# Attention and gated MLP on one core: fixed uses for the three transposition banks, weight conversions in other steps, the first x loaded two steps later

## The chip, the cores and the metric

The kernel runs on one core of a Trainium2 chip. The metric is the device time of one execution in microseconds. The core has five engines that run side by side and meet through semaphores: TensorE (PE in the profile; PEld are its weight loads), VectorE (DVE), ScalarE (ACT), GpSimd (POOL) and SyncE (SP), which here issues DMAs only.

## The reference

Attention over 4 batches, 8 heads, 576 positions and head dimension 64, with a bias that a small MLP makes of relative positions; then a gated MLP from 512 to 2048 and back over the 2304 tokens. All inputs are float32, except that the kernel is handed the two MLP weights as 64-bit words, which it converts on the chip.

```python
scores = scale * np.matmul(q, k.transpose(0, 1, 3, 2))
h = np.maximum(x @ w1 + b1, 0.0)            # x: psi_rel / psi_i
scores = scores + (h @ w2).transpose(2, 0, 1)[None, :, :, :]
attn = np.exp(scores - np.max(scores, axis=-1, keepdims=True))
attn = attn / (np.sum(attn, axis=-1, keepdims=True) + 1e-09)
attn_out = np.matmul(attn, v)
h = x @ w_in                                # x: attn_out as (2304, 512)
sp = np.where(h > 20.0, h, np.log1p(np.exp(np.minimum(h, 20.0))))
return (h * np.tanh(sp)) @ w_out
```

## The kernel before

The program has three stages: the bias (until some 56 us of the span), the attention loop (until some 287), and the MLP, in which TensorE is nearly always busy. The change touches the attention loop only.

The loop runs over 16 *pairs*: a pair `i` is one batch and two heads, which lie in the two halves of the 128 partitions. Each pair has five *steps*, one for each block of query rows, in the order 0, 1, 4, 2, 3 of `ORDER` (block 4 is half as long). Below, "first" to "fifth step" is the place in a pair, `x = n % 5` from 0 to 4 in the code; steps 0 to 79 are numbered `n`. Three steps are begun in the bias stage, so the loop proper starts with step 3. Code order is the order in which each engine executes: nothing reorders it (`tc.manual_schedule()`).

Work on one block is spread over several steps:

- `scores(n)`: TensorE, 12 matmuls into two score banks for each of the two heads (4 matmuls in the first three pairs, which are not split into high and low parts). The score banks hold one step only.
- `add_bias(n)`: VectorE, two passes that add the bias, write `pt` and leave the row minimum `m`; they free the score banks.
- `exps(n, u)`: ScalarE, one exponential per head (one for both in the third step, block 4), with the row sums.
- `ends(n)` and `transposes(n)`: TensorE turns `pt` around, 2 transpositions for the last 64 columns (`tail`) and 16 for the rest (`main`; 10 for block 4, which needs no `ends`). They go to `tp_t`, one PSUM tile of three banks. VectorE copies the tail out, ScalarE the two banks of `main` (lines 310, 313, 314).
- `products(n)`: TensorE, 20 matmuls of the transposed block with `v` into the bank `o`; after the second and the fifth block of a pair VectorE copies `o` to `x`, which a DMA writes to `x_d`.

`step(n)` issues `scores(n)`, `add_bias(n)`, `transposes(n-2)`, `exps(n)`, loads (`ahead`), `products(n-3)`, `ends(n-1)`, in a pair's first step the reciprocals of the pair before, and then `split(n)`. So TensorE has `ends(n-1)` right in front of `scores(n+1)`. Steps 3 and 4 are written out differently, as the first three blocks wait there to be transposed.

In `banks_of` the three banks of `tp_t` take turns: each call takes the next ones, so of the two banks that `ends` writes one is that of the first half of the last `transposes`, and the other lay idle.

`split(n)` calls `convert`, which takes one of four parts of a weight's conversion: a multiplication (line 125 on VectorE, or 123 on ScalarE if the weight starts in a third step), a shift (128), and two steps of bit arithmetic (130, 132). When a weight is done, the next is loaded, and the first four are also split in two at once (ScalarE line 142, then GpSimd line 143). Sixteen weights are converted in the loop, in 64 calls: one in each of steps 5 to 24, and later one in each step but the first of a pair.

GpSimd splits the q and k of the next pair (line 177, four subtractions) when their load has landed. In the last pair, `ahead` also makes the MLP's first x ready (lines 381 to 383): `load_x` and `load_r` bring the attention output and the reciprocals of the sums in steps 69 and 70, and steps 75 to 78 multiply them, on VectorE and GpSimd.

Of the kernel before, what the change touches and what calls it, by code (L numbers as in the profile page):

```python
# [7 lines left out]
F32 = mybir.dt.float32  # L8
# [7 lines left out]
B, H, S, D, C = 4, 8, 576, 64, 32  # L16
# [3 lines left out]
P = 128  # L20
# [25 lines left out]
def kernel(ctx: ExitStack, tc, qk, v, wb, w2, w_in, w_out, psia, psi4, rinv, eye, out):  # L46
# [42 lines left out]
    EARLY = 4  # L89
# [122 lines left out]
    NS = len(steps)  # L212
# [59 lines left out]
    def place(c):  # L272
        return (0, c * P) if c < 2 else (1, 0 if c == 4 else 64 + (c - 2) * P)

    tail_t, x_t, n_tp = {}, {}, [0]

    def banks_of(k):
        n_tp[0] += k
        return [(n_tp[0] - k + j) % 3 for j in range(k)]

    def ends(n):
        i, c = steps[n]
        tail_t[n] = tail = ptp.tile([P, P], F32, name="tail")
        if c == 4:
            return
        pt = live[n][0]
        t, l = sorted(banks_of(2))
        for rows, bank in ((TOP, t), (LOW, l)):
            pe.transpose(tp_t[:, bank, 0:64], pt[rows, 512:640], ident[rows, rows])  # L289
        dve.tensor_copy(tail.rearrange("p (g q) -> p g q", g=2), tp_t[:, t:l + 1:l - t, 0:64])  # L290

    def transposes(n, shared=False):
        i, c = steps[n]
        pt = live[n][0]
        main = ptp.tile([P, 2, 4, P], F32, name="main")
        pt_t[n] = main
        top, low = (tp_t[:, bank] for bank in banks_of(2))
        if c < 4:
            cols = [h * 640 + k * P for h in range(2) for k in range(4)]
        else:  # L300
            cols = [k * P for k in range(4)] + [S - P]
        for k, c0 in enumerate(cols):
            for rows, tp in ((TOP, top), (LOW, low)):
                if c == 4 and rows == LOW:
                    c0 = 64 + k * P if k < 4 else 0
                pe.transpose(tp[:, k * 64:k * 64 + 64], pt[rows, c0:c0 + P], ident[rows, rows])  # L306
        if c < 4:
            for g, tp in enumerate((top, low)):
                copy = dve.tensor_copy if shared and g else act.copy
                copy(main[:, :, :, 64 * g:64 * g + 64], tp.rearrange("p (h k q) -> p h k q", h=2, k=4))  # L310
        else:
            for h, tp in enumerate((top, low)):
                act.copy(main[:, h, :, 0:64], tp[:, :256].rearrange("p (k q) -> p k q", k=4))  # L313
                act.copy(tail_t[n][(TOP, LOW)[h], 0:64], tp[(LOW, TOP)[h], 256:320])  # L314

    def products(n):
        i, c = steps[n]
        hp, b = divmod(i, B)
        main, tail, vt = pt_t.pop(n), tail_t.pop(n), v_t[i]
        w = P if c < 4 else 64  # L320
        grp, off = place(c)
        if c in (0, 4):
            o_t[0] = o_ps.tile([P, 512], F32, name="o")
        o = o_t[0]
        for k in range(5):
            for h in range(2):
                pe.matmul(o[h * 64:h * 64 + 64, off:off + w], vt[:, h, k, :], main[:, h, k, :w] if k < 4 else tail[:, :w],  # L327
                          start=(k == 0), stop=(k == 4), skip_group_check=True)
        if c == 1:
            x = xs.tile([P, 320], F32, name="x")  # L330
            dve.tensor_copy(x[:, :256], o[:, :256])
            sp.dma_start(out=x_d[b][:, hp, 0:256], in_=x[:, :256])
        elif c == 3:
            x = xs.tile([P, 320], F32, name="x")
            dve.tensor_copy(x, o[:, :320])
            sp.dma_start(out=x_d[b][:, hp, 256:512], in_=x[:, 64:320])
            sp.dma_start(out=x_d[b][:, hp, 512:576], in_=x[:, 0:64])
# [27 lines left out]
    def ahead(n):  # L365
# [4 lines left out]
        c = {(1, 3): 0, (2, 1): 1, (2, 3): 2, (3, 2): 4, (3, 4): 3}.get((i % B, x))  # L370
        if c is not None and i // B + 1 < HP:
            load_bias(i // B + 1, c)
        if n == NS - 11:
            load_x(0, x0.tile([P, HP, TB], F32, name="xraw"))
        if n == NS - 10:
            x_hi[0], x_lo[0] = (xa_t[:, t].bitcast(F32R) for t in range(2))
            load_r(0, x_lo[0].bitcast(F32), 0, HP)
        if NS - 5 <= n < NS - 1:
# [2 lines left out]
            dve.tensor_tensor(hi, x, lo.bitcast(F32), op=ALU.mult)  # L381
            pool.tensor_tensor(x, x, lo.bitcast(F32), op=ALU.mult)
            pool.tensor_tensor(lo, x, hi.bitcast(F32), op=ALU.subtract)

    def split(n):

        i, x = divmod(n, 5)
        for _ in range((1 if n > 4 else 0)):
            convert(x == 2, order[EARLY + 11])

    done = []

# [10 lines left out]
    def step(n):  # L403
        i, x = divmod(n, 5)
        if n < NS:
            scores(n)
        if n == 3:
            ends(0)
            transposes(0, True)
        if n < NS:  # L410
            add_bias(n)
        if n == 4:
            products(0)
        if 4 <= n < NS + LAG:
            transposes(n - LAG)
        if n < NS:
            exps(n, 0)
            if n == 3:
                ends(1)
                transposes(1, True)  # L420
            exps(n, 1)
            ahead(n)
        if n >= 4:
            products(n - LAG - 1)
        if n <= NS:
            ends(n - 1)
        if n and x == 0 and n <= NS:
            reciprocals(i - 1)
        if n < NS and (x or i < 5):
            split(n)  # L430

# [428 lines left out]
```

## Time and profile before

| | |
|---|---|
| three runs | 669.90, 673.06, 673.11 us; median 673.06 |
| profiled execution | 671.56 us, its span 669.8 us |
| busy over the span | TensorE 635.8 us (95%), weight loads 530.0, VectorE 473.3, ScalarE 406.8, GpSimd 151.5 |
| granted TensorE clock, mean | 0.994 of full speed |
| attention loop, 104 to 270 us | TensorE 158.50, VectorE 139.82, ScalarE 145.96 busy of 166.00 |
| last pair, 270 to 290 us | TensorE 18.38, VectorE 17.66, ScalarE 14.12, GpSimd 10.74 busy of 20.00 |

Times in the profile count from the start of the span. Ends of matmuls are modelled, so a busy TensorE is not TensorE at its peak; the pitch from one step's instruction to the next step's is the surer measure. In the loop three engines are all near their limit, so the question at each place is which of them is waited for.

### The profile page before, as it was taken

The numbers are of one execution on the slowest core, as the hardware profiler recorded it, in microseconds if no ns is written. First come the engines' busy times: TensorE is split into PE (matmuls) and PEld (weight loads), VectorE is DVE, ScalarE is ACT, GpSimd is POOL, SyncE is SP. The second block draws the span as 40 slices with busy tenths as digits, with TensorE's granted clock in tenths as the row PEclk, the third lists the DMA queues.
The fourth block names the chain that finished last, engine by engine and source line by source line (L and its number), as shares of the span: only waits on it lengthen the run. The fifth ranks groups of instructions, "written<-read, shape, count | busy, mean of one in ns | idle before, by whom it ended". The sixth has DMA issues, their size and how long they took to land.

```text
span 669.8 us, 15502 instructions
## 1 busy us (share of the span) xinstructions
PE 635.8 (95%) x6132; PEld 530.0 (79%) x6132; DVE 473.3 (71%) x888; ACT 406.8 (61%) x805; POOL 151.5 (23%) x142
## 2 busy tenths in 40 slices
PE   5867999999999999999999999999999999999997
PEld 3214788888888888778888898888888888888886
DVE  7995788888888888924333536236489888888885
ACT  6894889888888888754333334244574444555441
POOL 0000133333222242422102112121253221333320
PEclk9988999999999999999999999999999999999999
DMA  4998486666578749114639687831765445424400
GB/s 146 310 308 252 154 266 207 208 220 210 181 228 255 238 163 273 52 41 144 204 103 268 235 230 210 251 126 66 249 189 157 151 148 154 135 95 129 135 31 32
DMA packets 101064, 119.76 MB, mean 179 GB/s; under 512 B 15616, under 2 KB 77568, under 8 KB 100992
## 3 DMA queue, kind: packets, MB, share of 16 engines
q1 hardware_dynamic: 98688, 110.59, 52.0%
q0 software_dynamic: 1872, 8.09, 4.0%
q8 instruction: 48, 0.79, 0.5%
q14 instruction: 24, 0.20, 0.1%
q10 hardware_dynamic: 432, 0.09, 0.1%
HBM read 79.47 MB, written 39.28 MB: 177 GB/s over the span
## 4 chain that ended last, share of the span: by engine, by line
PE 74%; ACT 7%; DVE 6%; issue 3%; DMA 2%; SPq 0%; ACTq 0%; DVEq 0%
PE h L587 28%; PE s L226 9%; PE y L708 8%; PE h L708 8%; PE o L327 7%; PE tp L306 5%; PE y L709 4%; PE h L709 4%; ACT main L310 3%; PE tp L289 2%; DVE pt L243 2%; ACT main L313 2%; DMA xlo<-r_d 1%; ACT tail L314 1%; DVE w L128 1%
## 5 line engine op out<-in xcount | busy, mean ns | idle before, releaser
L258 ACT ACTIVATE pt<-pt,m 128x576 f32<-128x576 f32 x144 | 111.3, 778 | 3.2 <-DVE m L243 2.7
L599 ACT ACTIVATE g<-h 128x512 f32<-128x512 f32 x72 | 42.9, 598 | 76.3 <-PE h L587 60.1
L243 DVE CUSTOM_DVE_ANT_0 pt<-s,bias 128x576 f32<-128x576 f32 (+1 forms) x112 | 81.3, 752 | 8.6 <-PE s L226 6.4
L310 ACT COPY main<-tp 128x512 f32<-128x512 f32 x126 | 67.8, 590 | 27.1 <-PE tp L306 25.1
L327 PE MATMUL o<-main,vt 128*64 128x128 f32 (+1 forms) x1280 | 81.9, 271 | 0.0
L603 POOL TENSOR_TENSOR g<-g 128x256 f32<-128x256 f32 (+1 forms) x40 | 34.1, 855 | 158.5 <-ACT g L599 149.4
L177 POOL TENSOR_TENSOR qklo<-rawqk,qkhi 128x304 fp32r<-128x304 f32 x52 | 44.6, 885 | 108.6 <-DMA rawqk<-in_qk_dram 108.6
L327 PEld LDWEIGHTS o<-main,vt 128*64 128x64 f32 x1280 | 64.1, 138 | 6.4 <-issue 1.1
L587 PE MATMUL h<-xa,lc 128*128 128x512 f32 (+1 forms) x288 | 55.8, 354 | 0.0
L306 PEld LDWEIGHTS tp<-ident,pt 64*128 64x128 f32 x1184 | 50.7, 139 | 4.8 <-DVE tail L290 2.6
L306 PE MATMUL tp<-ident,pt 64*128 64x64 f32 x1184 | 52.5, 222 | 2.1 <-DVE tail L290 2.1
L587 PEld LDWEIGHTS h<-xa,lc 128*128 128x128 f32 x288 | 47.6, 189 | 7.9 <-ACT g L599 0.5
L226 PE MATMUL s<-qkhi 64*128 64x288 f32 x260 | 51.1, 337 | 1.6 <-DVE m L243 1.4
L685 DVE TENSOR_TENSOR gslot<-quarters,gslot 128x1024 fp32r<-128x1024 f32 x28 | 47.1, 1706 | 7.3 <-ACT gslot L684 7.3
L684 ACT CAST gslot<-w 128x1024 fp32r<-128x1024 f32 x30 | 31.7, 1055 | 31.9 <-DVE w L681 18.8
L518 PE MATMUL bps<-ht,w2t 128*32 128x512 f32 (+17 forms) x352 | 36.5, 519 | 15.2 <-ACT bt L500 7.2
L685 DVE TENSOR_TENSOR gslot<-w,gslot 128x1024 fp32r<-128x1024 f32 x30 | 41.1, 1384 | 12.5 <-ACT gslot L684 12.5
L684 ACT CAST gslot<-quarters 128x1024 fp32r<-128x1024 f32 x28 | 29.6, 1058 | 31.4 <-DVE quarters L681 19.6
L488 DVE TENSOR_SCALAR ht<-at,bb 128x576 f32<-128x576 f32 (+17 forms) x123 | 44.1, 443 | 0.0
L226 PE MATMUL s<-qklo,qkhi 64*128 64x288 f32 x260 | 43.7, 296 | 0.0
L226 PE MATMUL s<-qkhi,qklo 64*128 64x288 f32 x260 | 42.3, 290 | 0.0
L518 PEld LDWEIGHTS bps<-ht,w2t 128*32 128x32 f32 x352 | 11.2, 117 | 39.1 <-ACT bt L500 27.0
(158 smaller groups left out, 1507.6 us busy)
## 6 DMA issues: line engine op xcount, KB each, us to landing
g_d<-g SPq DMA_DIRECT2D x32, 512.0 KB
bias_d<-bt SPq DMA_DIRECT2D x36, 295.5 KB
w<-in_w_in_dram SPq DMA_DIRECT2D x16, 512.0 KB
w<-in_w_out_dram SPq DMA_DIRECT2D x16, 512.0 KB
quarters<-g_d SPq DMA_DIRECT2D x16, 512.0 KB
qkhi<-in_qk_dram POOLq DMA_DIRECT2D x13, 608.0 KB, 4.4
rawqk<-in_qk_dram SPq DMA_DIRECT2D x13, 608.0 KB
w<-g_d SPq DMA_DIRECT2D x15, 512.0 KB
```

The lines of the kernel that those rows point to most:

```text
L226: pe.matmul(s[:, j, :SH], q[rows, c * P:(c + 1) * P], k[rows, KO + j * SH:KO + (j + 1) * SH], start=(t == 0), stop=(t == len(terms) - 1))
L243: dve.tensor_tensor_reduce(out=halves(pt[rows, sl]), in0=s[rows, :, :SH], in1=halves(bt[rows, sl]), scale=-0.125, scalar=BIG, op0=ALU.add, ...
L258: act.activation(ps, ps, AF.Exp, bias=m[:, u:u + 1], scale=-1.0, accum_out=sums[i][:, k:k + 1])
L306: pe.transpose(tp[:, k * 64:k * 64 + 64], pt[rows, c0:c0 + P], ident[rows, rows])
L310: copy(main[:, :, :, 64 * g:64 * g + 64], tp.rearrange("p (h k q) -> p h k q", h=2, k=4))
L327: pe.matmul(o[h * 64:h * 64 + 64, off:off + w], vt[:, h, k, :], main[:, h, k, :w] if k < 4 else tail[:, :w], start=(k == 0), stop=(k == 4) ...
L518: pe.matmul(ps[cg * 32:cg * 32 + 32, a:min(a + 512, n)], w2t, h_t[idx, cg][:, a:min(a + 512, n)], start=True, stop=True)
L587: pe.matmul(h[:, u * n:(u + 1) * n], w_at(f, d)[t], x[:, d, :n], start=(k == 0), stop=(k == 11))
L684: act.copy(hi, src)
L685: dve.tensor_tensor(lo, src, hi.bitcast(F32), op=ALU.subtract)
L708: pe.matmul(o, hi[:, f], wc[m][:, f], start=(f == 0 and m in (0, 1, 3)), stop=False, **kw)
L709: pe.matmul(o[:, 0:256], lo[:, f], wc[m][:, f, 0:256], start=False, stop=(f == 7), **kw)
```

## The change

`banks_of` is gone: `ends` always takes banks 1 and 2 of `tp_t`, `transposes` banks 1 and 0. For steps 0 and 1 `ends` takes bank 2 and, in place of a third bank, a tile of the `o` pool (`spare`), and comes behind `transposes` instead of ahead of it. The x copy moves out of `products` into `leave_pv`, which is issued behind `ends`. The conversions go by a table: in a pair's first step 1 (none from pair 9 on), in the second 1, in the third none, in the fourth 2, in the fifth 1, from step 5 to step 74; a weight starts on ScalarE if it starts in a second step. `load_x` and `load_r` of the first x are issued in steps 71 and 72.

```diff
-    def banks_of(k):
-        n_tp[0] += k
-        return [(n_tp[0] - k + j) % 3 for j in range(k)]
-    def ends(n):
+    def ends(n, spare=False):
...
-        t, l = sorted(banks_of(2))
-        for rows, bank in ((TOP, t), (LOW, l)):
-            pe.transpose(tp_t[:, bank, 0:64], pt[rows, 512:640], ident[rows, rows])
-        dve.tensor_copy(tail.rearrange("p (g q) -> p g q", g=2), tp_t[:, t:l + 1:l - t, 0:64])
+        tps = (tp_t[:, 2], o_ps.tile([P, 512], F32, name="o")) if spare else (tp_t[:, 1], tp_t[:, 2])
+        for rows, tp in zip((TOP, LOW), tps):
+            pe.transpose(tp[:, 0:64], pt[rows, 512:640], ident[rows, rows])
+        if spare:
+            for g, tp in enumerate(tps):
+                dve.tensor_copy(tail[:, 64 * g:64 * g + 64], tp[:, 0:64])
+        else:
+            dve.tensor_copy(tail.rearrange("p (g q) -> p g q", g=2), tp_t[:, 1:3, 0:64])
...
-        top, low = (tp_t[:, bank] for bank in banks_of(2))
+        top, low = tp_t[:, 1], tp_t[:, 0]
...
+    def leave_pv(n):            # the x copies and their DMAs, until now the end of products(n)
...
-        if n == NS - 11:
+        if n == NS - 9:
             load_x(0, x0.tile([P, HP, TB], F32, name="xraw"))
-        if n == NS - 10:
+        if n == NS - 8:
...
         if n == 3:
-            ends(0)
             transposes(0, True)
+            ends(0, True)
...
             if n == 3:
-                ends(1)
                 transposes(1, True)
+                ends(1, True)
...
             ends(n - 1)
+        if n >= 4:
+            leave_pv(n - LAG - 1)
         if n and x == 0 and n <= NS:
             reciprocals(i - 1)
-        if n < NS and (x or i < 5):
-            split(n)                     # convert(x == 2, order[EARLY + 11]) if n > 4
+        if 4 < n < NS - 5:
+            for _ in range((int(i < 9), 1, 0, 2, 1)[x]):
+                convert(x == 1, order[EARLY + 11])
```

VectorE in pair 10, from the shift of a weight behind the third step on. `pt` is written by `add_bias`, `x` and `tail` are the two copies. Before:

```order
L128 TENSOR_SCALAR w_3302<-w_3302 128x512
L243 ISA pt,m<-s,xraw 128x576
L243 ISA m 128x1
L243 ISA pt,m<-s,xraw 128x576
L243 ISA m 128x1
L130 SCALAR_TENSOR_TENSOR w_3732<-w_3732,w_3302 128x512
L243 ISA pt,m<-s,bias_2987 128x576
L243 ISA m 128x1
L243 ISA pt,m<-s,bias_2987 128x576
L243 ISA m 128x1
L331 COPY x<-o 128x256
L290 COPY tail<-tp 128x128
```

And after, from the second pass of the fourth step's `add_bias` on:

```order
L243 ISA pt,m<-s,xraw 128x576
L243 ISA m 128x1
L128 TENSOR_SCALAR w_3313<-w_3313 128x512
L130 SCALAR_TENSOR_TENSOR w_3743<-w_3743,w_3313 128x512
L243 ISA pt,m<-s,bias_2997 128x576
L243 ISA m 128x1
L243 ISA pt,m<-s,bias_2997 128x576
L243 ISA m 128x1
L290 COPY tail<-tp 128x128
L336 COPY x<-o 128x256
L132 SCALAR_TENSOR_TENSOR w_3743<-w_3313,w_3743 128x512
```

The shift of line 128 has moved from ahead of the fourth step's `add_bias` to behind it, next to line 130; the x copy stands behind the tail copy. Line 132 follows the last row in both.

ScalarE in the second and third step of a pair. Lines 310 are the copies of `main`, 258 the exponentials, `pt_` with a number is block 4. Before:

```order
L310 COPY main<-tp 128x8x64 x2
L258 ACTIVATE pt,sums<-pt,m 128x576 x2
L310 COPY main<-tp 128x8x64 x2
L258 ACTIVATE pt_3448,sums<-pt_3448,m 128x576
L310 COPY main<-tp 128x8x64 x2
```

And after:

```order
L310 COPY main<-tp 128x8x64 x2
L258 ACTIVATE pt,sums<-pt,m 128x576 x2
L123 ACTIVATE w_3442<-w_3094 128x512
L310 COPY main<-tp 128x8x64 x2
L258 ACTIVATE pt_3459,sums<-pt_3459,m 128x576
```

A weight's multiplication, line 123, now stands between the second step's exponentials and the third step's copies.

TensorE in step 3, with the semaphores that each row waits for (`DVE` is VectorE's, `Activation` ScalarE's). Lines 289 and 285 are those of `ends`, 306 that of `transposes`. Before:

```order
L289 MATMUL tp<-ident,pt 128x64 [waits DMAHW3_49,Activation_49]
L289 MATMUL tp<-ident,pt 128x64
L306 MATMUL tp<-ident,pt 128x64 [waits DVE_49]
L306 MATMUL tp<-ident,pt 128x64 x15
L289 MATMUL tp<-ident,pt 128x64 [waits DVE_49]
L289 MATMUL tp<-ident,pt 128x64
L306 MATMUL tp<-ident,pt 128x64 [waits DVE_49]
L306 MATMUL tp<-ident,pt 128x64 x15
L226 MATMUL s<-qklo 128x288 [waits PE_49] x2
```

And after:

```order
L306 MATMUL tp<-ident,pt 128x64 [waits DMAHW3_49,Activation_49]
L306 MATMUL tp<-ident,pt 128x64 x15
L285 MATMUL tp<-ident,pt 128x64 [waits DVE_49]
L285 MATMUL o<-ident,pt 128x64
L306 MATMUL tp<-ident,pt 128x64 [waits DVE_49]
L306 MATMUL tp<-ident,pt 128x64 x15
L285 MATMUL tp<-ident,pt 128x64 [waits DVE_49]
L285 MATMUL o<-ident,pt 128x64
L226 MATMUL s<-qklo 128x288 [waits PE_49] x2
```

The two sixteens have moved ahead of their `ends`, and the second `ends`, behind which the scores of step 4 stand, now waits for VectorE's copy of `main`. In an ordinary step nothing has moved here. The `ends` of a fifth step and the first scores of the next pair read, after:

```order
L285 MATMUL tp<-ident,pt 128x64 [waits Activation_49]
L285 MATMUL tp<-ident,pt 128x64
L226 MATMUL s<-qkhi 128x288 [waits DMASW6_49,DVE_49]
L226 MATMUL s<-qkhi 128x288 [waits DVE_49]
L226 MATMUL s<-qklo,qkhi 128x288 [waits Pool_49]
L226 MATMUL s<-qklo,qkhi 128x288
L226 MATMUL s<-qkhi,qklo 128x288 [waits Pool_49]
L226 MATMUL s<-qkhi,qklo 128x288
L226 MATMUL s<-qkhi 128x288 x2
L226 MATMUL s<-qklo,qkhi 128x288 x2
L226 MATMUL s<-qkhi,qklo 128x288 x2
L306 MATMUL tp<-ident,pt 128x64 [waits DVE_49]
```

The waits are the same as before: `ends` for ScalarE, the sixteen for VectorE.

## Rows read from the trace of the kernel before

**Rows 1.** Waits from 112 to 270: engine, line, waited for; us, times, longest us.

```profile
PEld tp L289 <- ACT main L310: 10.7, 33, 0.9
...
PEld s L226 <- DVE m L243: 3.0, 11, 0.4
...
PEld s L226 <- issue: 1.0, 6, 0.2
```

**Rows 2.** Timeline of an ordinary step: start us, us, engine, line, operation, idle before.

```profile
203.83 0.28 PE L289 MATMUL tp<-ident,pt 64*128 64x64 f32 x2
...
205.10 0.19 ACT L258 ACTIVATION_READ_ACCUMULATOR pt<-pt,m 128x1 f32 x1
...
205.50 1.07 ACT L310 COPY main<-tp 128x512 f32<-128x512 f32 x2 [0.20 <-PE tp L306]
...
206.63 0.14 PEld L289 LDWEIGHTS tp<-ident,pt 64*128 64x128 f32 x2 [0.17 <-ACT main L310]
```

**Rows 3.** Timeline of pair 10's fourth and fifth steps, where the scores wait.

```profile
206.54 3.42 POOL L177 TENSOR_TENSOR qklo<-rawqk,qkhi 128x304 fp32r<-128x304 f32 x4 [8.86 <-DMA rawqk<-in_qk_dram]
...
207.47 1.00 DVE L128 TENSOR_SCALAR w<-w 128x512 uint32<-128x512 uint32 x1
...
208.39 0.75 DVE L243 CUSTOM_DVE_ANT_0 pt<-s,xraw 128x576 f32<-128x576 f32 x1
...
209.87 0.18 PEld L226 LDWEIGHTS s<-qkhi 64*128 64x128 f32 x1 [0.27 <-DVE m L243]
```

**Rows 4.** Durations of lines 128 and 123, 100 to 290: ns minimum/median/maximum.

```profile
L128 DVE TENSOR_SCALAR w<-w x13: 423/999/1141, 108.7 to 281.4; 128x512 uint32<-128x512 uint32 x13
...
L123 ACT ACTIVATE w<-w x1: 672/672/672, 106.8 to 106.8; 128x512 f32<-128x512 f32 x1
```

**Rows 5.** Timeline from pair 10's fifth step to pair 11's second.

```profile
212.54 0.42 DVE L331 COPY x<-o 128x256 f32<-128x256 f32 x1 [0.24 <-PE o L327]
...
212.98 0.29 DVE L290 COPY tail<-tp 128x128 f32<-128x128 f32 x1
...
213.18 0.68 DVE L132 SCALAR_TENSOR_TENSOR w<-w,w 128x512 uint32<-128x512 uint32 x1
...
213.78 0.75 DVE L243 CUSTOM_DVE_ANT_0 pt<-s,xa 128x576 f32<-128x576 f32 x1
...
215.40 0.14 PEld L289 LDWEIGHTS tp<-ident,pt 64*128 64x128 f32 x2 [0.57 <-ACT main L310]
```

**Rows 6.** Timeline of VectorE in pair 3's first step, with a conversion.

```profile
101.38 0.66 DVE L130 SCALAR_TENSOR_TENSOR w<-w,w 128x512 uint32<-128x512 uint32 x1
...
101.95 0.76 DVE L243 CUSTOM_DVE_ANT_0 pt<-s,xa 128x576 f32<-128x576 f32 x1
```

**Rows 7.** Timeline of step 3.

```profile
57.09 0.71 PE L306 MATMUL tp<-ident,pt 64*128 64x64 f32 x16 [0.45 <-DVE tail L290]
...
57.90 0.59 ACT L310 COPY main<-tp 128x512 f32<-128x512 f32 x1 [1.57 <-PE tp L306]
...
58.51 0.69 DVE L310 COPY main<-tp 128x512 f32<-128x512 f32 x1 [1.48 <-ACT main L310]
...
59.91 0.78 ACT L258 ACTIVATE pt<-pt,m 128x576 f32<-128x576 f32 x1 [1.43 <-DVE m L243]
...
61.37 1.94 PE L226 MATMUL s<-qklo 64*128 64x288 f32 x8
```

**Rows 8.** Waits from 270 to 288, the last pair.

```profile
PEld s L226 <- DVE m L243: 1.3, 3, 0.6
...
PEld tp L306 <- DVE tail L290: 0.6, 1, 0.6
```

**Rows 9.** Timeline of SyncE and VectorE around the first x.

```profile
258.15 1.32 SPq L361 DMA_DIRECT2D xa<-r_d  x2
...
272.42 0.69 DVE L381 TENSOR_TENSOR xa<-xraw,xa 128x512 fp32r<-128x512 f32 x1
...
273.28 1.22 DVE L265 TENSOR_SCALAR sums<-sums 128x9 f32<-128x9 f32 x1
```

More of the change, by code (lines that the diff above doesn't have):

```diff
@@ L273, in place @@
         return (0, c * P) if c < 2 else (1, 0 if c == 4 else 64 + (c - 2) * P)
-    tail_t, x_t, n_tp = {}, {}, [0]
-    def banks_of(k):
-        n_tp[0] += k
-        return [(n_tp[0] - k + j) % 3 for j in range(k)]
-    def ends(n):
+    tail_t = {}
+    def ends(n, spare=False):
         i, c = steps[n]
@@ L328, in products @@
                           start=(k == 0), stop=(k == 4), skip_group_check=True)
+    def leave_pv(n):
+        i, c = steps[n]
+        hp, b = divmod(i, B)
+        o = o_t[0]
         if c == 1:
@@ L383, in ahead @@
             pool.tensor_tensor(lo, x, hi.bitcast(F32), op=ALU.subtract)
[L385 to L389, printed above, removed]
     done = []
```

## The prediction

> **What bounds the kernel now.** I read the waits of the attention loop first, then one step on the timeline, then the few steps that take longer, and last the two ends of the loop. The two times of the profiled execution are 669.8 us of span and 671.56 us in all, so 1.76 us lie around the span; all sums below are made against that execution.
>
> Between 112 and 270 us (eleven head pairs, five steps each) TensorE idles for two reasons [rows 1]. The first transposition of `ends` waits for ScalarE's copy of the banks: 10.7 us in 33 waits. The scores wait for VectorE's `m`, which is `add_bias` of the step before leaving the score banks: 3.0 us in 11 waits, and 1.0 us more in 6 short gaps named "issue" at the same scores.
>
> An ordinary step shows how the first wait makes a circle [rows 2]. `ends` starts at 203.83, the scores and the sixteen transpositions follow, ScalarE's two copies of `main` start at 205.50 and take 1.07, and the next `ends` starts at 206.63, right behind the second copy at 206.57. So the period is 2.80 us, and a delay of ScalarE's copies delays the next step by as much. ScalarE has little to spare here: its last read of the sums ends at 205.29, the copies start at 205.50, 0.21 later.
>
> The second wait sits at one place, the fifth step of a pair [rows 3]. A conversion (line 128) starts at 207.47 behind the tail copy and takes 1.00, because GpSimd's subtractions run from 206.54 to 209.96; alone this instruction takes 0.42 [rows 4]. `add_bias` starts at 208.39, and the second score matmul can start only at 209.87, 1.48 later: two passes of 0.75, a little overlapped.
>
> **The change part by part.**
>
> *Fixed banks.* The waits decide, not the bank numbers. In the changed program the first transposition of `ends` still waits for ScalarE and the first of the sixteen still for VectorE (the rows of the order above). In the trace `ends` starts 0.06 behind the second copy [rows 2], although with turns too one of its banks is the old free one and the other is left by the first copy. So the tile is waited for as a whole: 0.0. The price if that is wrong stands with the rivals.
>
> *Tail copy ahead of the x copy.* Behind the third step there is now no conversion, so nothing is late there. Behind the fifth, `x` used to be copied at 212.54, while VectorE waited for `ends` anyway; the tail came at 212.98, line 132 at 213.18 and `add_bias` at 213.78 [rows 5]. Now the tail keeps its place, the x copy adds its pitch behind it (0.42 less some 0.1 of overlap, 0.33), and line 132 and `add_bias` come 0.33 later. `add_bias` let the second score matmul go at 213.78 + 1.48 = 215.26; it stands behind `ends`, which starts at 215.40 [rows 5], so it is wanted at some 215.5 and there are 0.24 to spare. Of the 0.33 some 0.1 is lost, with bounds of 0 and 0.33. It counts where line 130 or 132 lies in a fifth step: ten pairs, +1.0.
>
> *Conversions that start on ScalarE.* Before, one weight of the loop starts there, in a third step, where ScalarE has one exponential instead of two. Now eight do, all behind the second step's two exponentials and ahead of the next copies. Line 123 takes 0.67 [rows 4], with an overlap of 0.1 as above and the 0.21 of spare time of rows 2 taken off: 0.36 each. One of the eight follows a step that is late anyway (first-step slot of pair 8, below); 7 x 0.36 = +2.5. Bounds: 0 if the copies are not delayed, 0.67 each if nothing hides, 5.4. I take 2.5 as the circle of rows 2 has no other slack. The Trainium skill (Perfetto Trace Analysis, Optimizing Scalar/DVE Operations) says that moving work from a saturated VectorE to ScalarE may make sense. By that rule the term would be 0 and the sum 2.5 lower; the rows show that in this step ScalarE is the fuller engine.
>
> *Two conversions in the fourth step.* Behind `add_bias` of the fourth step there is no tail and no x copy, and the scores of the fifth step, 0.9 long, are computed before VectorE is wanted again; with the 0.24 to spare that makes room for about 1.5 us. Two conversions of 0.42 to 0.68 fit, 1.36 at most. Line 128 may still meet the last of GpSimd's subtractions, as in rows 3, where they end at 209.96. I take nothing for it except where a weight's split follows on GpSimd (pair 4): +0.3, bounds 0 and 3 (0.3 in each of ten pairs).
>
> *First-step slots.* Pairs 5 to 8 now have a conversion there too, behind the reciprocals. How that looks is shown at 101.38: line 130 sits there, and `add_bias` starts at 101.95, 0.57 later than without it [rows 6]. A heavy one (lines 130, 132, two cases) costs 0.57 - 0.24, some 0.35, a light one of 0.42 (two cases) 0.1: +0.9, bounds 0.2 and 1.4.
>
> *The third- and fifth-step stalls that go.* Line 128 leaves the third step, so `add_bias` of the fourth is on time: the 3.0 + 1.0 of rows 1 go, -4.0. Bound: 0 if the double slot brings them back.
>
> *Last pair.* It has no conversions now. Before, the scores there wait 1.3 for VectorE and the transpositions 0.6 for the tail copy [rows 8], 1.9 together. Line 265, which takes 1.22 at 273.28 beside GpSimd's multiplication, is no conversion and stays [rows 9]. So not all goes: -1.5, bounds -1.9 and 0.
>
> *First x two steps later.* Its second part (`load_r`) was issued at 258.15 and used at 272.42 without a wait [rows 9], 14.3 us later. Two steps are 5.6, which leaves 8.7 us; its megabyte and the one of `load_x` then follow the pair's loads instead of preceding them. I count 0, and +1.0 as the upper bound if VectorE must wait.
>
> *Start of the loop (step 3).* Before: transpositions of step 0 at 57.09 behind `ends`, ScalarE's copy 57.90, VectorE's 58.51, exponential 59.91, and the scores of step 4 at 61.37 [rows 7]. Now the sixteen come first, at 56.4; 0.71, then ScalarE's copy from about 57.3 (0.59), VectorE's 0.69 until 58.65. `ends` waits for that copy (rows of the order), and VectorE's first tail copy follows 0.38 later, at 59.1; the second sixteen wait for it and run 59.4 to 60.1. But now ScalarE does the exponential of step 3 before the second copy: `add_bias` from 59.4, exponential 60.2 to 61.0, copy to 61.6, VectorE's copy to 62.3, and only then `ends`, behind which the scores of step 4 are queued: 62.5 instead of 61.37. +1.2 with the latencies, bounds 0 (TensorE catches up before pair 1) and 2.0 (one more exponential, 0.78, gets in front of a copy).
>
> Sum: 1.0 + 2.5 + 0.3 + 0.9 + 1.2 - 4.0 - 1.5 = +0.4 us. The pairs before number 4 lose and gain less than I can read. On the profiled execution that is 672.0; the median of the three runs is 673.06, 1.5 above that execution, and one run is 669.9. I take the middle of 672.0 and 673.5: 672.7.
>
> **The rivals.**
>
> *The fixed banks free `ends`.* If `ends` waited for the first copy alone, the 10.7 us of rows 1 over eleven pairs would go, and as much in the other pairs: about 1.0 x 13.5 = 13 us less, 660. For it: the first copy leaves the bank 0.5 before the second. Against it: the order's rows and the 0.06 of rows 2. The Trainium skill (PSUM — Partial Sum Buffer, Summary: rules for kernel authors) says that PSUM being read while matmuls run wants a different bank; by that rule this rival would hold, but the trace shows waiting across banks.
>
> *The new places cost nothing.* ScalarE's starts, the x copy and the slots are all hidden, and only the gains and the start remain: 1.2 - 4.0 - 1.5 = -4.3 in place of +0.4, so 668.0. For it: VectorE does 0.42 less in each of eight pairs. Against it: 0.21 of spare time on ScalarE.
>
> *Slower: ScalarE becomes the bound.* The eight starts delay the copies by their whole 0.67, since `exps` of the step before end later as soon as the copies are late once: 5.4 instead of 2.5, 675.6. It decides from the point at which the copies behind a line 123 start more than 0.5 later than without it (1.67 us behind their `ends` in rows 2). Against it: the third step has one exponential, so ScalarE catches up within a step.
>
> **How the numbers follow.** Forecast 0.74, its own range 670.7 to 674.7 (the start, ScalarE's starts and the last pair each off by a third of their bounds). Free banks 0.03, nothing costs 0.12, ScalarE bound 0.11. A change of 0.5% (3.4 us) is about what a measurement of this kernel can tell from none. Faster by more: 0.03 + most of 0.12 and a little of the forecast, 0.14; slower by more: 0.11, as a delayed load or start would have to join; same 0.75. The range leaves out free banks and the outer part of the two other rivals: 669.2 to 676.2.
>
> **What would show it.** In the profile after: `ends` still starts within 0.1 of the second copy; the scores of step 4 start near 62.5; line 123 stands eight times before 270 us, each followed by copies some 0.36 late; the scores' wait for `m` between 112 and 270 falls from 3.0 to under 1.5; the stretch from step 75 to the first `hidden` is 1.5 shorter; VectorE doesn't wait for `load_r`. I am wrong if `ends` starts between the two copies, if a step with line 123 keeps 2.80, or if the fifth steps still take over 3.1.

## The result and the profile after

The changed kernel takes 676.82 us (median of 14 executions, 673.31 to 680.39) against 672.93 before (14 executions): a ratio of 1.0059, 95% interval 1.004 to 1.0079, some 4.0 us slower. My 672.7 was 4.1 too low, and the range ended at 676.2. Ratios leave out an execution that lies over 1.5% above the fastest of its kernel, which happens once below, in a_split. The changed kernel's profiled execution has 674.1 us of span and 675.9 in all, against 669.8 and 671.56.

The gap between the two profiled executions can be walked through by the starts of the scores and of the first `hidden`, which is the first matmul of the MLP:

| stretch | before | after | difference |
|---|---|---|---|
| scores of step 3 start at | 54.96 | 54.73 | -0.2 |
| steps 3 and 4 | 12.32 | 13.80 | +1.5 |
| steps 5 to 19 (pairs 1 to 3) | 44.57 | 44.42 | -0.2 |
| steps 20 to 74 (pairs 4 to 14) | 158.12 | 158.13 | 0.0 |
| scores of step 75 to the first `hidden` | 16.75 | 17.33 | +0.6 |
| first `hidden` to the last pair of a 512- and a 256-column matmul of the projections | 376.64 | 379.26 | +2.6 |

Up to step 74 this is nearly what I forecast (+1.9, measured +1.1), though that rests on the one execution from which I took the stalls, as the second executions below show. The last two rows are not: I had -1.5 and 0.

The waits from 112 to 270 us after the change answer to [rows 1]:

```profile
PEld tp L285 <- ACT main L310: 12.4, 33, 0.9
...
PEld s L226 <- DVE m L243: 2.2, 13, 0.2
```

`ends` still waits for ScalarE's copies, as often as before, and a little longer. The scores' wait for `m` fell from 3.0 only to 2.2, where I had given under 1.5 as a sign, and it sits elsewhere: the longest is 0.2 and not 0.4.

The third step of pair 10, timeline (the step with line 123; it answers to [rows 2]):

```profile
204.99 0.14 PEld L285 LDWEIGHTS tp<-ident,pt 64*128 64x128 f32 x2 [0.17 <-ACT main L310]
...
206.34 0.68 ACT L123 ACTIVATE w<-w 128x512 f32<-128x512 f32 x1
...
206.92 1.06 ACT L310 COPY main<-tp 128x512 f32<-128x512 f32 x2
...
208.02 0.14 PEld L285 LDWEIGHTS tp<-ident,pt 64*128 64x128 f32 x2 [0.41 <-ACT main L310]
```

The copies start 1.93 behind their `ends` instead of 1.67, and the next `ends` comes 3.03 later instead of 2.80, within 0.1 of the end of the second copy. So `ends` was not freed, and a start on ScalarE costs 0.25 here.

The fifth step of the same pair and the second of the next, timeline (it answers to [rows 3] and [rows 5]):

```profile
210.55 0.42 DVE L128 TENSOR_SCALAR w<-w 128x512 uint32<-128x512 uint32 x1
...
211.91 0.76 DVE L243 CUSTOM_DVE_ANT_0 pt<-s,bias 128x576 f32<-128x576 f32 x1 [0.21 <-PE s L226]
...
214.12 0.41 DVE L336 COPY x<-o 128x256 f32<-128x256 f32 x1
...
214.45 0.68 DVE L132 SCALAR_TENSOR_TENSOR w<-w,w 128x512 uint32<-128x512 uint32 x1
...
215.05 0.75 DVE L243 CUSTOM_DVE_ANT_0 pt<-s,xa 128x576 f32<-128x576 f32 x1
...
216.34 0.14 PEld L285 LDWEIGHTS tp<-ident,pt 64*128 64x128 f32 x2 [0.57 <-ACT main L310]
```

Line 128 and line 130 lie in the fourth step without harm: VectorE even waits 0.21 for the scores. The second wait of `m` moved behind line 132: `add_bias` starts 1.29 before `ends`, where it was 1.62 before, and needs 1.48 for its first part.

Step 3, timeline (it answers to [rows 7]):

```profile
56.14 0.71 PE L306 MATMUL tp<-ident,pt 64*128 64x64 f32 x16 [0.17 <-ACT bt L502]
...
58.72 0.27 PE L285 MATMUL tp<-ident,pt 64*128 64x64 f32 x1 [1.87 <-DVE main L310]
...
60.87 0.56 ACT L310 COPY main<-tp 128x512 f32<-128x512 f32 x1
61.33 0.77 ACT L258 ACTIVATE pt<-pt,m 128x576 f32<-128x576 f32 x1
61.46 0.69 DVE L310 COPY main<-tp 128x512 f32<-128x512 f32 x1 [0.73 <-ACT main L310]
...
62.37 1.28 PE L226 MATMUL s<-qklo 64*128 64x288 f32 x4
```

This is the chain of the prediction, with step 4's scores at 62.37 (forecast 62.5). What I had not followed is TensorE's clock. Windows of both kernels (us of the window; TensorE, its weight loads, VectorE, ScalarE, GpSimd busy; granted clock; share of the DMA engines; GB/s), first before, then after:

```profile
60.00:62.00 2.00, 1.19 (x20) 1.13 (x22) 0.76 (x3) 1.22 (x3) 0.00 (x0) 0.92 0.56 177
62.00:64.00 2.00, 2.00 (x14) 1.10 (x12) 1.36 (x2) 0.92 (x3) 0.00 (x0) 0.50 0.89 230
64.00:66.00 2.00, 2.00 (x30) 1.76 (x28) 0.87 (x4) 0.08 (x1) 0.00 (x0) 0.73 0.94 310
```

```profile
58.00:60.00 2.00, 0.96 (x15) 0.83 (x16) 1.64 (x6) 0.00 (x0) 0.00 (x0) 0.84 0.60 207
60.00:62.00 2.00, 0.42 (x8) 0.23 (x6) 1.27 (x5) 1.91 (x4) 0.00 (x0) 0.50 0.47 142
62.00:64.00 2.00, 1.79 (x10) 1.29 (x10) 0.51 (x3) 0.20 (x2) 0.00 (x0) 0.50 0.90 273
64.00:66.00 2.00, 2.00 (x18) 1.46 (x16) 1.36 (x4) 0.00 (x0) 0.00 (x0) 0.50 0.94 348
66.00:68.00 2.00, 2.00 (x38) 1.76 (x36) 0.08 (x2) 0.81 (x3) 0.00 (x0) 0.95 0.17 68
```

A granted clock of 0.50 is 1.2 GHz; 0.84 over two microseconds means 0.64 us of them at half speed. So the half-speed stretch is 3.4 us long before (61.7 to 65.1) and 6.8 after (59.4 to 66.2), behind more idle time of TensorE around step 3. Up to 70 us the two kernels are level here, with 6.8 us at half speed each, because the kernel before has another such stretch near 40 us, as the pages' clock rows show, before and then after (tenths, slices of some 16.8 us, the third and fourth from the left):

```profile
PEclk9988999999999999999999999999999999999999
```

```profile
PEclk9997999999999999999999999999999999999999
```

The last pair, timeline of SyncE and VectorE (it answers to [rows 9]), and its waits (they answer to [rows 8]):

```profile
259.69 2.37 SPq L183 DMA_DIRECT2D vt<-in_v_dram  x1
262.15 1.37 SPq L270 DMA_DIRECT2D r_d<-rt  x4
263.56 0.57 SPq L352 DMA_DIRECT2D xraw<-x_d  x1
264.18 1.75 SPq L366 DMA_DIRECT2D xa<-r_d  x2
...
275.49 0.69 DVE L386 TENSOR_TENSOR xa<-xraw,xa 128x512 fp32r<-128x512 f32 x1 [1.54 <-issue]
```

```profile
PEld tp L306 <- DVE tail L290: 2.2, 2, 1.6
DVE xa L386 <- issue: 1.5, 1, 1.5
PEld s L226 <- DVE m L243: 1.0, 3, 0.5
```

VectorE waits 1.54 for the first x, and behind it stands the tail copy for which TensorE waits 1.6. "Issue" means that the profile shows no releaser; the profile of b_loads names it below.

### The profile page after: what moved, and what is told of

Read it like the earlier page. It is cut to its first block, busy times and chain, and to the rows that moved or that the text cites. A ratio compares the mean times of both kernels' runs of the same rounds, so it can differ in the third digit from the quotient of the medians.

```text
span 674.1 us, 15501 instructions
## 1 busy us (share of the span) xinstructions
PE 636.4 (94%) x6132; PEld 530.1 (79%) x6132; DVE 465.7 (69%) x883; ACT 407.8 (60%) x812; POOL 148.3 (22%) x142
## 4 chain that ended last, share of the span: by engine, by line
PE 69%; ACT 14%; issue 3%; DVE 3%; DMA 3%; SPq 0%; ACTq 0%; DVEq 0%
PE h L589 29%; PE y L710 8%; PE h L710 8%; PE s L226 7%; ACT main L310 6%; ACT pt L258 4%; PE y L711 4%; PE h L711 4%; PE tp L306 4%; PE o L327 3%; PE tp L285 2%; ACT main L313 2%; DMA xa<-r_d 1%; DMA rawqk<-in_qk_dram 1%; ACT tail L314 1%
## 5 line engine op out<-in xcount | busy, mean ns | idle before, releaser
L177 POOL TENSOR_TENSOR qklo<-rawqk,qkhi 128x304 fp32r<-128x304 f32 x52 | 42.0, 833 | 108.8 <-DMA rawqk<-in_qk_dram 108.8
L226 PE MATMUL s<-qkhi 64*128 64x288 f32 x260 | 49.6, 338 | 0.4 <-DVE m L243 0.4
L290 DVE COPY tail<-tp 128x128 f32<-128x128 f32 x62 | 18.1, 292 | 34.8 <-PE tp L285 29.4
```

Source lines behind the costliest of these rows:

```text
L226: pe.matmul(s[:, j, :SH], q[rows, c * P:(c + 1) * P], k[rows, KO + j * SH:KO + (j + 1) * SH], start=(t == 0), stop=(t == len(terms) - 1))
```

## The experiments

Each ratio below has its interval. The difference of two of them is uncertain by some 2 us (an estimate, from the two intervals taken together), so the steps of the profiles have to carry what smaller differences of times can't.

**Three parts undone, one at a time.** First the loads of the first x:

```diff
-        if n == NS - 9:
+        if n == NS - 11:
             load_x(0, x0.tile([P, HP, TB], F32, name="xraw"))
-        if n == NS - 8:
+        if n == NS - 10:
```

> The changed kernel, with the loads of the first x back in steps 69 and 70. In the changed kernel VectorE waited 1.54 us for them in step 75, and from the scores of step 75 to the first `hidden` it took 17.33 us, against 16.75 before. Theory (the late load eats what the last pair gains): that stretch becomes 15.3 to 15.8, VectorE does not wait, the first `hidden` starts near 286.6 instead of 288.42, and the time falls by some 1.5 to 2.0 to about 675.0. Rival (the last pair is held by the line-265 addition beside GpSimd, and the load hides): the stretch stays above 17 and the time at 676.8. On the projections (960 matmuls in 490 pairs, 346.7 ns a pair from 514 us on before and 353.1 in the changed kernel): if the program sets that pace, it is 353 here; if it is settled anew in each execution, it may be either.

Ratio to before 1.0029 (1.0006 to 1.0052), 2.0 us less than the change, with an uncertainty as large. In the profile VectorE doesn't wait, the stretch takes 15.74 and the first `hidden` starts at 286.39: the theory's numbers. The other direction, these two lines alone put into the kernel before:

> The kernel before, with only the loads of the first x moved to steps 71 and 72. Theory (late load): VectorE waits 1.5 to 2 us in step 75, the stretch from the scores of step 75 to the first `hidden` grows from 16.75 to 18.3 to 18.8, time 672.9 + 1.5 to 2.0 = 674.4 to 674.9. Rival (the wait needs the other changes, as in the changed kernel the pair's loads stand 1 us later): below 0.5 more, 673.4 at most. Pace of the projections: 346.7 if the program's attention code sets it and the load has no part in it, either if it is settled anew.

Ratio 1.0017 (0.9996 to 1.0038): slower by 1.1 at best guess, which the interval doesn't part from nothing. The profile does: the stretch takes 19.15, more than expected, and here the profile names what VectorE waits for:

```profile
272.97 0.69 DVE L381 TENSOR_TENSOR xa<-xraw,xa 128x512 fp32r<-128x512 f32 x1 [2.35 <-DMA xa<-r_d]
```

Next the starts on ScalarE:

```diff
-                convert(x == 1, order[EARLY + 11])
+                convert(False, order[EARLY + 11])
```

> The changed kernel, with every weight of the loop started on VectorE (line 125) instead of ScalarE (line 123) in a pair's second step. Theory (the copies behind line 123 are late by 0.25 us in each of nine pairs, as the trace of the changed kernel shows, 3.05 against 2.80): the nine steps fall back to 2.80, 2.0 to 2.3 us less in all, time about 674.6. Rival (VectorE is as full there: the 0.42 of line 125 delays the next add_bias instead): the steps fall by less than 0.1 each or the ones behind them grow, time 676.3 to 677.5. Pace of the projections: 353 if the program sets it, either if not.

Ratio 1.0031 (1.0007 to 1.0055), 1.9 less, again no more than its uncertainty. The third steps of pairs 9 to 14 take 2.80 instead of 3.03 to 3.05. Some of it comes back: in pairs 11 to 13 a first step grows to 2.96 or 3.26, where VectorE does what ScalarE did. Pairs 4 to 14 take 156.41, 1.7 less. Then step 3:

```diff
+            ends(0)
             transposes(0, True)
-            ends(0, True)
...
+                ends(1)
                 transposes(1, True)
-                ends(1, True)
```

> The changed kernel, with step 3 in the order of before (`ends` of steps 0 and 1 ahead of their transpositions, banks 1 and 2 as in the other steps). Theory (the new order keeps TensorE idle longer: 7.64 us from the scores of step 3 to those of step 4, against 6.41, and its clock at half speed for 6.8 us after it, against 3.4): the scores of step 4 start 1.0 to 1.3 earlier, the half-speed stretch near 60 us has its 3.4 us again, and the time falls by 1.0 to 1.6, to 675.2 to 675.8. Rival (the clock falls once more elsewhere, as in the kernel before at 37 to 41 us, and takes it back): time 676.3 to 677.3.

Ratio 1.0049 (1.0024 to 1.0074), 0.7 less. Steps 3 and 4 take 12.29, as before the change. The half-speed stretch near 62 is short again, but others lie at 38 to 42 and 48 to 52 in this execution. Up to 70 us TensorE is at half speed for 6.8 or 10.2 us in all in the kernels with one tile of three banks, in either order of step 3, and with the order of before steps 3 and 4 also took 13.33 (b_table) and 13.40 (a_all_x). So what the new order costs is not shown by the times.

**All three undone** (the three diffs above together), and then the order of the copies too:

> The changed kernel with three of its parts undone together: loads of the first x in steps 69 and 70, conversions started on VectorE, step 3 in the order of before. What stays of the change: the fixed banks, the x copy behind the tail copy, the conversions in other steps. Theory (those three parts are what made it slower: 1.2 at the start, 2.2 in nine steps, 2 in the last pair and its clock): 676.8 - 5.4 = 671.4, which is 1.5 faster than before. Rival (what stays costs too, the gains in the fifth steps being smaller in most executions than in the profiled one: 2.0 instead of 4.0): 672.5 to 673.5, no different from before.

Ratio 0.9991 (0.9969 to 1.0013), 4.6 less than the change: the sum of the three (2.0 + 1.9 + 0.7), as the theory adds them, and the one difference of these that is clear of its uncertainty. But the kernel is no faster than before, as the rival says.

```diff
             products(n - LAG - 1)
+            leave_pv(n - LAG - 1)
         if n <= NS:
             ends(n - 1)
-        if n >= 4:
-            leave_pv(n - LAG - 1)
```

> The kernel of a_all with the x copy ahead of the tail copy again, so that of the change only the fixed banks and the conversions' places stay. Theory (the x copy behind the tail copy makes add_bias late, 0.12 in nine second steps): the second steps fall from 2.92 to 2.80, pairs 4 to 14 from 156.0 to 155.0, time 672.5 - 1.0 = 671.5. Rival (line 132 makes it late, the order of the two copies doesn't matter): 2.92 stays, time 672.5.

Ratio 0.9963 (0.9938 to 0.9989): 2.5 us faster than before, and 1.9 less than a_all, which the intervals don't part from nothing. All second steps but pair 4's are 2.80, so the order of the two copies made the 0.12 (in seven pairs of a_all, not nine), and line 132 alone does not. Pairs 4 to 14 fall only to 155.77 and not to 155.0, as first steps take 0.5 more and third steps 0.2.

**The table alone**, in the kernel before:

```diff
-        if n < NS and (x or i < 5):
-            split(n)
+        if 4 < n < NS - 5:
+            for _ in range((int(i < 9), 1, 0, 2, 1)[x]):
+                convert(x == 1, order[EARLY + 11])
```

> The kernel before, with only the table of conversions of the changed kernel (none in the last pair, starts on ScalarE in the second step). Theory (the table alone: fifth steps 2.6 to 4.2 less, third steps 2.4 more, first steps 0.5 more, last pair 1.0 less as in a_loads): pairs 4 to 14 take 157.0 (158.1 with the x copy's 1.0 in the second steps, which is not in this kernel), the stretch from step 75 to the first `hidden` 15.7; time 671.0 to 672.5. Rival (the second steps' 0.12 comes from line 132 and the table, not from the x copy): pairs 4 to 14 take 158.1 and the time is 673.

Ratio 1.0004 (0.9981 to 1.0026): no difference. Pairs 4 to 14 take 156.75, the last stretch 15.79, second steps 2.80 (pair 4's apart): as the theory has it. The time, 672.91, lies above the theory's 672.5, at the rival's 673.

**Both kernels a second time.**

> The kernel before, unchanged, in a second execution. In the first its fifth steps of pairs 4 to 14 took 4.2 us more than 2.82 each; in b_loads, whose loop is the same up to step 71, 2.6. Theory (the stall depends on when GpSimd's subtractions fall on line 128, and so on the landing of a transfer, and varies between executions): 2 to 4 us here, and pairs 4 to 14 together 156.5 to 158.1. Rival (4.2 is the rule and b_loads the exception, through its later loads): 4.0 to 4.4. The stretch from the scores of step 75 to the first `hidden`: 16.75 as before in either case.

Below the theory's range: the fifth steps take 1.4 more than 2.82 each, pairs 4 to 14 together 155.35. So 4.2, 2.6 and 1.4 in three executions of the same loop; the rival falls. The last stretch is 16.74 again. The step's length follows that of line 128, which lies beside GpSimd's subtractions nearly always. In b_again it took 0.43 to 0.45 beside them in four pairs, and those fifth steps took 2.81 or 2.82; where it took 1.00 and 1.09 they took 3.26 and 3.33. What makes it short or long beside them is not shown.

> The changed kernel, unchanged, in a second execution. Theory (the late load is a race that comes out otherwise each time): step 76, which took 4.82 us there and 4.9 to 8.3 in the kernels that load as late, takes 4.8 to 8.5, and where it takes more than 5.5 the clock of TensorE is at half speed behind it for 5 to 8 us; the stretch from step 75 to the first `hidden` is then 18 to 20.5 instead of 17.33. Rival: 4.8 again and no half speed. Projections at 346.6 or 353.1 ns a pair.

As the theory: step 76 takes 7.59, the stretch 19.10, the whole 678.9. VectorE waited 3.25 for the load. Only the half-speed stretch is shorter than the theory's 5 to 8 us: 3.4. Windows of this execution:

```profile
276.00:278.00 2.00, 0.26 (x5) 0.03 (x1) 0.00 (x0) 0.49 (x2) 0.00 (x0) 1.00 0.52 193
278.00:280.00 2.00, 0.65 (x16) 0.65 (x16) 1.59 (x3) 0.00 (x0) 0.82 (x1) 0.90 0.05 19
280.00:282.00 2.00, 2.00 (x23) 1.88 (x23) 1.93 (x6) 1.43 (x3) 1.72 (x2) 0.50 0.01 1
282.00:284.00 2.00, 2.00 (x30) 1.67 (x30) 1.26 (x5) 1.28 (x4) 1.02 (x1) 0.74 0.02 2
```

TensorE is busy 0.26 and 0.65 of two microseconds each, and then works at half speed from 279.6 to 283.0. That added next to nothing: the stretch less VectorE's wait is 15.85, against 15.79 in the first profile, which has no half speed here (17.33 less 1.54), and 15.74 in a_loads, which has no wait. In b_loads, with 3.4 us at half speed, it is 16.80 (before: 16.75). Only in a_nudge and a_split, with 6.8 us at half speed, it is 0.9 more, 16.69 and 16.70.

The loop in the profiles with one tile of three banks, pairs 4 to 14, as excess over 2.80, 2.80, 2.80, 2.71 and 2.82 a step, summed over eleven pairs (fourth steps have none), and the last stretch:

| | first | second | third | fifth step | pairs 4 to 14 | step 75 to `hidden` |
|---|---|---|---|---|---|---|
| before | 0.1 | 0.7 | 0.0 | 4.2 | 158.12 | 16.75 |
| b_again | 0.0 | 0.7 | 0.0 | 1.4 | 155.35 | 16.74 |
| b_loads | 0.0 | 0.7 | 0.0 | 2.6 | 156.55 | 19.15 |
| b_table | 0.3 | 0.7 | 2.7 | -0.1 | 156.75 | 15.79 |
| after | 0.6 | 1.7 | 2.4 | 0.3 | 158.13 | 17.33 |
| a_again | 0.6 | 1.7 | 2.4 | 0.3 | 158.20 | 19.10 |
| a_loads | 0.4 | 1.5 | 2.4 | 0.3 | 157.71 | 15.74 |
| a_start | 0.6 | 1.6 | 2.6 | 0.0 | 157.96 | 17.48 |
| a_nudge | 0.9 | 1.5 | 2.4 | 0.2 | 158.22 | 20.52 |
| a_noact | 1.2 | 1.3 | 0.7 | 0.0 | 156.41 | 17.76 |
| a_all | 0.5 | 1.6 | 0.7 | 0.0 | 156.04 | 16.00 |
| a_all_x | 1.1 | 0.7 | 0.9 | -0.1 | 155.77 | 15.86 |

**The projections.** From 514 us to the end each pair of a 512- and a 256-column matmul takes 346.7 ns before and 353.3 after (the mean distance of the starts of the 512-column ones), though nothing there was changed and the granted clock is 1.00 in both. To see whether the program sets this, the changed kernel got cuts:

```diff
...
+        cut = {2: (256, 512), 3: (384, 512), 4: (128, 512), 5: (256, 384, 512), 6: (256, 512), 7: (320, 512)}.get(p)
+            if m == 0 and f == 4 and cut:      # this one matmul of 512 columns in two or three pieces
...
```

> The changed kernel, where in six of the nine tiles of the projections one matmul of 512 columns is cut into two or three (tile 2: 256+256, tile 3: 384+128, tile 4: 128+384, tile 5: 256+128+128, tile 6: 256+256, tile 7: 320+192 columns); the rest of the instructions is the same. The profiles so far have a pair of projection matmuls at 346.6 ns (the kernel before, a_loads, a_noact) or at 353.1 (the changed kernel, b_loads, a_split) through all of 440 pairs from 514 us on, though none of these kernels differs there. Theory (TensorE settles in one of two rhythms at the 1 us stop near 508 us and stays in it, so a disturbance of the rhythm can change it): the pace changes at one or more of the six cuts, between 346.6 and 353.1. Rival (something else that lasts through an execution sets the pace, such as the clock): one pace throughout. Time: 676.8 in either case, less 2.9 x the share of tiles at the other pace.

The theory holds: 353.3 until the first cut at 537 us, 346.8 behind it and behind the next three, 353.2 from the fifth (615) to the sixth (634), 346.7 behind that. Two timelines of this execution, before and behind the first cut; the distance of the 512-column starts is 0.35 and 0.34, and it takes the mean over many pairs to see the sizes:

```profile
518.38 0.40 PE L715 MATMUL y<-combo,gslot 128*128 128x512 f32 x1
...
518.73 0.40 PE L715 MATMUL y<-combo,gslot 128*128 128x512 f32 x1
...
538.17 0.39 PE L715 MATMUL h<-combo,gslot 128*128 128x512 f32 x1
...
538.51 0.39 PE L715 MATMUL h<-combo,gslot 128*128 128x512 f32 x1
```

And the kernel before shows both: 346.7 in its first profile, 353.3 in b_again. So one program can run at either pace, and some 2.9 of the 4.3 us between the two profiled spans need no change of the program. Whether a change shifts how often each pace comes is not shown: the times of the unprofiled executions don't tell their pace. Time of a_nudge: 1.0049 (1.002 to 1.0077).

**Three PSUM tiles instead of one**, to see what the fixed banks are worth:

```diff
-        tps = (tp_t[:, 2], o_ps.tile([P, 512], F32, name="o")) if spare else (tp_t[:, 1], tp_t[:, 2])
+        tps = (tp_t[2], o_ps.tile([P, 512], F32, name="o")) if spare else (tp_t[1], tp_t[2])
...
+        for g, tp in enumerate(tps):          # one tail copy of 64 columns for each bank
+            dve.tensor_copy(tail[:, 64 * g:64 * g + 64], tp[:, 0:64])
...
-        top, low = tp_t[:, 1], tp_t[:, 0]
+        top, low = tp_t[1], tp_t[0]
...
-    tp_t = lpsum("t_ps", 1).tile([P, 3, 512], F32, name="tp")
+    t_ps = lpsum("t_ps", 3)
+    tp_t = [t_ps.tile([P, 512], F32, name="tp") for _ in range(3)]
```

> The changed kernel, with the three transposition banks as three PSUM tiles instead of one tile of three banks, and with two tail copies of 64 columns in place of one of 128. Then the first transposition of `ends` waits for ScalarE's first copy only, not for the second. Theory (waiting by whole tile hides the use of fixed banks; behind it ScalarE is next, whose two copies and two exponentials follow one another in 2.60 us of a step of 2.80): steps of 2.62 to 2.72 in place of 2.80, 5 to 10 us less, time 667 to 672. Rival 1 (my prediction's rival, nothing else holds): 1.0 us for each of the waits shown, 13 us less, 664. Rival 2 (the second tail copy makes VectorE late, or PSUM is held anyway): no step shorter than 2.78, time 676 to 679.

Ratio 0.9876 (0.9841 to 0.9911); the median of all six executions, 665.76 us, lies between the theory's range and rival 1. The one left out of the ratio, 673.72 us, is the profiled one: there VectorE waited 2.50 for the first x. Its pairs 4 to 14 take 153.43, 0.43 less each than after the change. The loop is read from the next kernel, with the three parts undone as well:

> The kernel of a_all (loads, starts and step 3 as before) with the three transposition banks as three PSUM tiles. In a_split `ends` stood behind ScalarE's first copy and the pairs took 0.35 us less each, but the first x came 4 us too late in the last pair, after which TensorE's clock was at half speed for 7 us. Theory (the gain of the split adds to those of undoing the three parts): 665.8 - 5.4 = 660.4, between 658 and 663. Rival (VectorE, which has two tail copies now and the conversions' starts too, becomes the bound: the second steps of a pair, already 3.0 to 3.4 in a_split, grow to 3.4 to 3.8): 664 to 667.

Ratio 0.9882 (0.9849 to 0.9916), 665.02 us: in the rival's range, though not by the rival's sign, as the second steps didn't grow beyond the 3.0 to 3.4 of a_split. Pairs 4 to 14 take 153.07, 3.0 less than in a_all, and steps 3 to 14 another 3.2. Waits from 105 to 262, and the window:

```profile
PEld s L226 <- DVE m L243: 5.5, 23, 0.5
PEld tp L285 <- ACT main L307: 3.8, 22, 0.2
...
105.00:262.00 157.00, 155.78 (x2734) 140.34 (x2730) 139.63 (x421) 140.14 (x341) 46.86 (x58) 1.00 0.70 227
```

The wait for ScalarE fell from 12.4 us (10.6 in a_all) to 3.8, VectorE's `m` took its place (second steps of 3.0 to 3.4), and TensorE is busy in 99% of this window. Most first steps take 2.3 to 2.7 and fifth steps 2.63, while third and fourth steps stay near 2.80 and 2.71. Undoing the three parts gains nothing clear on a_split, as the intervals overlap; why, no run shows. Both kernels beat the kernel before by 1.2%. Three tiles that take turns, as the banks did before, were not tried, so what the tiles give without the fixed uses is open. The Trainium skill (PSUM — Partial Sum Buffer, Summary: rules for kernel authors) says that PSUM which is read while matmuls run wants another bank, with semaphores bank by bank. With one tile the bank alone bought nothing; with a tile for each bank the traces agree with the rule.

## Why the prediction was wrong

**First x: the step that failed.** I wrote "I count 0, and +1.0 as the upper bound". Issue and use of `load_r` were 14.3 us apart, and I let 8.7 remain without asking how long the load takes. The DMA view of the kernel before had it (256 to 276 us in 40 slices of 0.5):

```profile
DMA  9999999999999999999999730000007095793000
GB/s 427 409 389 343 338 365 339 376 388 370 346 383 380 228 235 213 217 234 246 225 202 214 185 104 14 4 0 0 0 0 258 4 66 172 295 410 139 0 0 2
```

The engines are full until some 268. The trace has the packets themselves: those of 2048 bytes belong in this stretch to `load_x` and `load_r` alone, and the last of them ended at 267.90, 9.75 us behind the issue of `load_r` at 258.15. In the fourteen profiles it is 9.75 to 13.0. So 8.7 was too little. I also had `load_r` ahead of the pair's loads, and SyncE's rows show it right behind them; only `load_x` stood ahead:

```profile
251.62 0.57 SPq L347 DMA_DIRECT2D xraw<-x_d  x1
...
257.56 0.54 SPq L183 DMA_DIRECT2D vt<-in_v_dram  x1
```

In the new place `load_x`, a second megabyte, is issued 0.6 ahead of `load_r`, both behind the write of `r_d` on SyncE. After the change the last packet ended at 274.59, 10.4 behind the issue at 264.18, and VectorE had been ready since 273.95. In all seven profiles of kernels that load late the multiplication starts 0.6 to 1.6 us behind the last packet, also where the profile says "issue". VectorE waited 1.54 to 3.83 in them, and the stretch was 17.33 to 20.52 where a_loads, a_all, a_all_x and b_table have 15.74 to 16.00. That is 1.5 to 4.7 us in place of 0, in a profile; by the times 2.0, with an uncertainty as large.

**Fifth-step stalls: right place, wrong size.** They go, as forecast, all but one (pair 12, 3.10). But the 4.0 were those of one execution; three give 4.2, 2.6 and 1.4, mean 2.7, and 0.3 stays, so the gain is 2.4. A stall that varies so between executions needed a range of its own.

**How the miss adds up.** This is an estimate from the few profiles of the two kernels and b_loads, without the projections, whose pace differs between executions. Pairs 4 to 14 take 1.5 more than the mean of the three old loops, where my terms came to +0.7. Steps 3 and 4 take 1.5 and 2.2 more, for +1.2. The last stretch takes 0.6 and 2.4 more, for -1.5: it lies 2.1 and 3.9 above its terms and holds most of the 3.6 us between my sum of +0.4 and the measured 4.0.

**The other terms.** `ends`: 0.0, as forecast. ScalarE's starts: 2.5 forecast; of the 2.4 in the third steps 1.7 go without the starts, seven times 0.25 where I had 0.36. The x copy: 1.0, and 1.0 in the second steps. First steps: 0.9, and 0.5, but in pairs 4 and 6 alone, where I had counted four slots in pairs 5 to 8, while the 0.7 that stays in the third steps of pairs 6 to 8 had no term and no run takes it apart; that the sum comes near is luck. The fourth step's double slot: 0.3, and 0. The start: 1.2, and 1.2 from step 3's scores to step 4's, 1.5 with step 4, which runs at half speed. The last pair without the load gives -1.0 in a_loads, in its bounds, not my -1.5.

**The rivals.** `ends` was not freed. ScalarE did not become the bound: the copies are 0.26 late, not 0.5 or more. "Nothing costs" fell with the third steps. The slower outcome came mostly from the load, which I had as a bound and not as a rival, though it had a place, a price and a point of decision: the landing of `load_r` against step 75.

**What I took for noise.** The two paces of the projections part two executions of one kernel by 2.9 us, about what I called no change. The profiled execution before had the shorter one, the one after the longer.

## What to carry to other kernels

Before a load is moved later, read when it landed, not when it was issued, and add what is now queued ahead of it. A wait in front of the next stage is paid in full here, and TensorE's fall to half speed behind it added 0.1 us or 0.9, far less than its length. A stall that depends on a landing is worth its mean over several executions, not what one profile shows. Fixed uses of PSUM banks gained nothing while one tile spanned them; with a tile for each bank the kernel is 1.2% faster than before.

## What the runs showed of the hardware

TensorE showed two steady rhythms for the same stream of alternating 512- and 256-column matmuls at full clock, 346.7 and 353.3 ns a pair. Behind the 1 us stop near 508 us it ran in one and kept it to the end, and in a_nudge three of six cut matmuls changed it. Four profiles had the shorter and nine the longer (a_nudge both). What in TensorE makes the two, and what picks one, stays open.

Behind the wait for the first x TensorE's clock fell to half speed in four of the seven profiles that have the wait: step 76 took 6.27, 7.06, 7.59 and 8.34 us there (b_loads, a_split, a_again, a_nudge), and 4.82, 4.88 and 5.27 in the three others (after, a_start, a_noact).
